# A convolution and top-2 mixture of experts on one core: opening rebuilt with a banded convolution, expert matmuls in 64-row pairs, and planned costs of GpSimd and of the row data changed

## The chip, the core and the metric

The kernel runs on one core of one Trainium2 chip, in one launch. The metric is the device time of an execution in microseconds (us). TensorE is called PE in the profile (its weight loads PEld), VectorE DVE, ScalarE ACT, GpSimd POOL and SyncE SP.

## The reference, cut to what matters

```
w   = softmax(weight, over the 7 taps)                 # 8 heads x 7 taps; a head is 24 of the 192 channels
xc  = causal convolution of x with w, per head         # x: 8 x 3584 x 192 f32, so N = 28672 tokens of D = 192
noisy = xc @ w_gate + log1p(exp(xc @ w_noise)) * noise # N x 8 experts
top2  = two largest of noisy, gates = softmax of those two
for e in range(8):                                     # F = 1024
    for each token that has e among its top two:
        out[token] += gate * (relu(xc[token] @ w1[e]) @ w2[e])
```

All inputs and outputs are f32. The kernel runs the expert matmuls in f16 on split operands: each value is scaled by a power of two and written as a high and a low f16 part, and three products (high by high, high by low, low by high) are summed in f32.

## The kernel before, in words

**Units.** The tokens fall into 28 units of 1024. In a unit each of the 128 partitions holds 8 neighbouring tokens, with the six tokens before them as the halo of the convolution. For each unit `load_x` (L278) brings 768 KB, `conv` (L545) makes xc, takes the largest absolute value of each row (L575), scales the rows by a power of two (L579) and writes the high and low parts into one of two row buffers `rb`, 400 f16 wide. `gating` (L594) then turns the rows into columns (on PE through the py buffers for the first five units, L613, by transposing DMAs for the others), multiplies them with the gate weights (the logits, L637, into the PSUM tile misc), and on DVE goes through some thirty small instructions of 64 columns: softplus, noise, two rounds of maximum and one-hot. M (L702) is the sum of both one-hots. PE ranks the rows of each expert with it (L709 and the two behind), DVE makes the row indices (idx, L747) and writes the gates into the row buffers. Last, `scatters` (L759) has GpSimd write the 1024 rows twice, in 16 indirect DMAs of 128 rows (L768), into a DRAM table xs that has a region for each expert.

**The convolution of the first units.** Units 0, 1 and 2 are convolved on PE (`conv_pe`, L501): one f32 matmul of 128 x 128 by 192 columns for each of 7 taps and each head (half of the heads of unit 0), with diagonal matrices `dg` that `diagonals` (L489) makes beforehand on DVE and ACT. ACT copies the result from PSUM (L569). All other units take DVE: a multiply and six multiply-adds for each of 8 heads, 56 instructions of 128 x 192 (L560, L562).

**Blocks.** A round takes the next rows of every expert: first a round of 128 rows, then 28 rounds of 256. A block is one expert in one round, so there are 232 blocks, of which 224 have 256 rows. For a block SP issues two transposing loads from xs (bT, three buffers; `block_loads`, L891). PE runs `mm1` (L848): for each half of F, 16 matmuls of 128 rows and 256 columns into a ph buffer (there are two), and four matmuls of 64 rows, which take the low part of the last 64 channels, at the end of the first half and at the start of the second. ACT writes the high part of the relu into h (L854), DVE the low part (`relu_low`, L858), and then ph is free. PE runs `mm2` (L866): for each 128 of the rows 24 matmuls of 192 columns into a py buffer (two). ACT scales by the gate (L872, y, six buffers), and GpSimd adds the rows to the output with an indirect DMA (L877). PE's order is mm1 of block n, then mm2 of block n-1. The row numbers and gates of a round come back from xs (`load_meta`, `round_meta`).

**What sets the order.** Each engine runs its instructions in the order in which the program lists them, and that list is written by a planner (class `Plan`, L46). The work is written as threads; a thread says `yield ENGINE, cost` before it emits instructions, and `run` (L90) always takes the thread whose start on the planned clock, less its urge, is smallest. The costs are written by hand: 1.05 for a scatter, 1.6 for an add, 0.33 for a conv step, 1.0 + 0.15 for a relu_low, 2.0 for an mm2 half. Rings (L499) stand for the buffers: 2 ph, 2 py, 6 y, 3 bT. Urges come from due times (L520 to L543). Semaphores, which keep the data right, are set independently of the plan.

**The opening.** Weights of expert 0 come first, then x of unit 1 and the other experts' weights in turn. Each expert's weights are scaled by a factor from the diagonal of their gram matrix (L364, matmuls into grams) and split in two (L412). The output is zeroed by 28 DMAs from SP (L432), one per unit. A block waits in the plan until every unit whose rows it may hold has scattered (`ready_unit`, L157).

Of the kernel before, what the change touches and what calls it, by code (L numbers as in the profile page):

```python
# [8 lines left out]
F32 = mybir.dt.float32  # L9
# [9 lines left out]
P = 128  # L19
# [26 lines left out]
class Plan:  # L46
# [7 lines left out]
    GAP = 0.1  # L54

    def __init__(self, **clock):
        self.clock, self.threads, self.now = clock, [], 0.0
# [32 lines left out]
    def run(self):  # L90
        self.spawned = []
        while True:
            best = None
            for th in self.threads:
# [3 lines left out]
                at = max(self.clock[eng], th[0] + (self.GAP if th[4] != eng else 0.0))  # L98
# [5 lines left out]
                urge = th[3](at) if callable(th[3]) else th[3]  # L104
                if best is None or at - urge < best[0]:
                    best = at - urge, at, th
# [18 lines left out]
def kernel(  # L125
# [22 lines left out]
    BIG = 2 * P  # L148
    assert D == 192 and E == 8 and I % TU == 0 and P % B == 0 and S % I == 0 and U > 3
# [28 lines left out]
    start = tc.tile_pool(name="start", bufs=1)  # L178
    spool = start.__enter__()
# [24 lines left out]
    def iota_f(name, shape, pattern, base, mult):  # L204
        t = const.tile(shape, I32, name=name + "_i")
        nc.gpsimd.iota(t, pattern=pattern, base=base, channel_multiplier=mult)
# [3 lines left out]

    tok0 = iota_f("tok0", [P, TU], [[1, TU]], 0, I)
    rowp = iota_f("rowp", [P, 2], [[P, 2]], 0, 1)
# [12 lines left out]

    runs = const.tile([P, U + 1, E], F32, name="runs")
# [3 lines left out]
    def pow2(mx, n, t, name):  # L230
# [8 lines left out]
        V.tensor_scalar(f, f, -1, 254, op0=OP.mult, op1=OP.add)  # L239
        V.tensor_scalar(i, f, 23, None, op0=OP.logical_shift_left)  # L240
        return s.bitcast(F32), i.bitcast(F32)
# [35 lines left out]

    def load_x(u):  # L278
        xt = xpool.tile([P, HALO + TU, D], F32, name="xt")
        xts[u] = xt  # L280
        if u:
            nc.sync.dma_start(xt[:, HALO:, :], dview(xf, u * TU * D, [[I * D, P], [D, TU], [1, D]]))
        else:
            for p0, p1 in ((16, P), (1, 16)):
# [781 lines left out]
```

## Time and profile before

| | before |
|---|---|
| median of 3 runs (lowest to highest) | 2117.39 us (2103.3 to 2119.4) |
| profiled execution | 2097.99 us |
| its span, first to last instruction | 2096.2 us |
| granted clock of PE, mean | 0.978 |
| busy: PE | 1983.7 us (95%) in 21703 matmuls |
| busy: DVE | 1565.0 us (75%) |
| busy: POOL | 1271.8 us (61%) |
| busy: ACT | 803.3 us (38%) |
| L848, mm1 | 9280 matmuls |
| L866, mm2 | 10944 matmuls |
| L858, relu_low | 557.5 us in 464 |
| L768, scatters | 494.2 us in 448 |
| L877, adds | 776.0 us in 456 |

How to read it: the profile is one execution. Busy time is the sum of what an engine's instructions lasted, so an engine can be busy 95% of the span and yet be held up in one part of it; the views by stretch show where. Matmuls overlap one another in the array, and a row of PE is a run of matmuls with its start, its length and their number. An idle time is written in brackets with what ended it: "<-DVE h L858" is a wait for a result, "<-issue" a time in which the engine waited for nothing that the trace shows. The granted clock is the share of its full clock that PE got.

### The profile page before, as it was taken

The page shows a single profiled execution, that of the slowest core. Times are in us where ns is not written, and L with a number is a line of the kernel's source. Part 1 is how long each engine was busy: PE and PEld are TensorE (multiplying, and loading weights), DVE is VectorE, ACT ScalarE, POOL GpSimd, SP SyncE. Part 2 cuts the span into 40 slices and gives each one's busy share as a digit, 9 for nine tenths or more (in the row PEclk, how much of TensorE's full clock was granted, in tenths as well). Part 3 has the DMA queues.
Part 4 walks back from the last instruction along what each step waited for, and adds up shares of the span by engine and source line. Part 5 has one row for each costly group of instructions (what it writes and reads, how often), then busy time and mean ns, then how long its engine had stood idle before and what let it go on. Part 6 is the DMA issues. An engine that isn't in the chain of part 4 may idle for free.

```text
span 2096.2 us, 52494 instructions
## 1 busy us (share of the span) xinstructions
PE 1983.7 (95%) x21703; PEld 1778.0 (85%) x21703; DVE 1565.0 (75%) x4042; ACT 803.3 (38%) x1173; POOL 1271.8 (61%) x915
## 2 busy tenths in 40 slices
PE   7557999999999999999999999999999999999997
PEld 6546888878888899889899998988898888999986
DVE  6677888878888898889988888889899753333232
ACT  4334343333334343443343434433443433333332
POOL 0353576765666776777667777777767665333333
PEclk9778999999999999999999999999999999999999
DMA  8733456876657677666777766677777664444442
GB/s 238 196 91 79 86 98 118 155 148 118 117 92 125 130 132 128 122 126 117 118 129 133 126 130 117 113 120 131 130 132 115 107 98 77 58 61 57 60 58 35
DMA packets 521882, 236.99 MB, mean 113 GB/s; under 512 B 401304, under 2 KB 508824, under 8 KB 521505
## 3 DMA queue, kind: packets, MB, share of 16 engines
q1 hardware_dynamic: 433824, 142.72, 33.2%
q0 software_dynamic: 87200, 90.80, 29.3%
q8 instruction: 171, 2.80, 0.6%
q14 instruction: 79, 0.65, 0.1%
q10 hardware_dynamic: 608, 0.02, 0.0%
HBM read 40.12 MB, written 115.38 MB: 74 GB/s over the span
## 4 chain that ended last, share of the span: by engine, by line
PE 88%; DVE 5%; issue 3%; SPq 2%; ACT 1%; DMA 1%; another core or an unknown queue 0%; ACTq 0%; POOL 0%; DVEq 0%; POOLq 0%
PE ph L848 43%; PE py L866 41%; PE ph L514 1%; SPq L622 1%; PE misc L637 1%; DVE h L858 1%; PE grams L364 1%; DVE xc L562 0%; DMA xT<-rb 0%; DVE w1s L412 0%; SPq L911 0%; DVE w2s L412 0%; PE py L613 0%; DVE t L673 0%
## 5 line engine op out<-in xcount | busy, mean ns | idle before, releaser
L877 POOL DMA_INDIRECT out_dram<-y,ids x456 | 776.0, 1702 | 593.2 <-ACT y L872 423.5
L848 PE MATMUL ph<-bT,w1s 128*128 128x256 f16 (+2 forms) x9280 | 1004.7, 273 | 26.6 <-issue 10.3
L866 PE MATMUL py<-w2s,h 128*128 128x192 f16 x10944 | 953.1, 246 | 12.0 <-issue 11.3
L848 PEld LDWEIGHTS <-w1s 128*128 128x128 f16 (+1 forms) x9280 | 773.2, 98 | 210.6 <-issue 116.6
L866 PEld LDWEIGHTS <-h 128*128 128x128 f16 x10944 | 910.0, 98 | 23.8 <-issue 18.3
L858 DVE SCALAR_TENSOR_TENSOR h<-ph,h 128x1024 f16<-128x1024 f32 (+1 forms) x464 | 557.5, 1203 | 389.8 <-ACT h L854 345.2
L854 ACT ACTIVATE h<-ph 128x1024 f16<-128x1024 f32 (+1 forms) x464 | 468.0, 1009 | 556.8 <-PE ph L848 469.1
L768 POOL DMA_INDIRECT xs<-rb,idx x448 | 494.2, 1103 | 212.7 <-issue 144.7
L562 DVE SCALAR_TENSOR_TENSOR xc<-xt,wt,xc 128x192 f32<-128x192 f32 x1224 | 422.9, 410 | 3.3 <-DMA xt<-zero 3.3
L872 ACT ACTIVATE y<-py,ga 128x192 f32<-128x192 f32 x456 | 191.5, 421 | 602.2 <-PE py L866 439.2
L514 PE MATMUL ph<-xt,dg 128*128 128x192 f32 x280 | 50.8, 339 | 14.9 <-DMA xt<-in_x_dram 11.6
L514 PEld LDWEIGHTS ph<-xt,dg 128*128 128x128 f32 x280 | 47.3, 197 | 15.3 <-DVE dg L494 11.5
L560 DVE TENSOR_SCALAR xc<-xt,wt 128x192 f32<-128x192 f32 x204 | 53.9, 330 | 1.2 <-DMA xt<-in_x_dram 0.5
L575 DVE TENSOR_REDUCE am<-xc 128x8 f32<-128x1536 f32 x28 | 49.0, 1752 | 4.4 <-ACT xc L569 3.7
L579 DVE TENSOR_TENSOR xc<-xc,xs 128x1536 f32<-128x1536 f32 x28 | 49.3, 1761 | 0.0
L637 PE MATMUL misc<-gparts,xT 128*128 128x32 f16 (+1 forms) x752 | 27.4, 175 | 16.7 <-issue 15.3
L673 DVE SCALAR_TENSOR_TENSOR t<-t,t 128x64 f32<-128x64 f32 x168 | 38.1, 227 | 5.7
L637 PEld LDWEIGHTS <-xT 128*128 128x128 f16 x752 | 24.4, 97 | 19.8 <-issue 17.6
L589 DVE TENSOR_TENSOR rb<-xc,rb 128x1024 f16<-128x1024 f32 x28 | 34.1, 1217 | 4.3 <-ACT rb L585 2.1
L585 ACT ACTIVATE rb<-xc 128x1024 f16<-128x1024 f32 x28 | 29.5, 1053 | 11.1 <-DVE xc L579 9.3
L483 ACT ACTIVATE xt<-xt 128x1152 f32<-128x1152 f32 x27 | 31.2, 1156 | 0.0
L719 DVE TENSOR_REDUCE sums<-M 128x72 f16<-128x576 f16 x23 | 27.0, 1172 | 0.0
(142 smaller groups left out, 620.0 us busy)
## 6 DMA issues: line engine op xcount, KB each, us to landing
out_dram<-zero SPq DMA_DIRECT2D x28, 768.0 KB
xt<-in_x_dram SPq DMA_DIRECT2D x27, 768.0 KB
bT<-xs SPq DMA_TRANSPOSE x464
out_dram<-y,ids POOLq DMA_INDIRECT x456
xs<-rb,idx POOLq DMA_INDIRECT x448
w2s<-in_moe_w_dram SPq DMA_DIRECT2D x16, 384.0 KB
w1s<-in_moe_w_dram SPq DMA_DIRECT2D x8, 512.0 KB
w1s<-in_moe_w_dram SPq DMA_DIRECT2D x16, 256.0 KB
```

Of the source, the lines that this page charges most:

```text
L514: nc.tensor.matmul(c[:, h - h0, :TU * G].rearrange("p (t g) -> p t g", g=G), diag[h, k], xts[u][:, k:k + TU, h * G:(h + 1) * G], start=(k ...
L560: V.tensor_scalar(dst, src, wt[:, h, k:k + 1], None, op0=OP.mult)
L562: V.scalar_tensor_tensor(dst, src, wt[:, h, k:k + 1], dst, op0=OP.mult, op1=OP.add)
L579: V.tensor_tensor(xc, xc, xsc[:, :, None].to_broadcast([P, TU, D]), op=OP.mult)
L637: nc.tensor.matmul(lg[:, t], xT[:, t, c, :], g[:, gc], start=(i == 0), stop=(i == len(seq) - 1))
L768: s = nc.gpsimd.indirect_dma_start(out=xsf, out_offset=bass.IndirectOffsetOnAxis(ap=idx[:, k, t:t + 1], axis=0), in_=rbf[:, t, :], in_offs ...
L848: nc.tensor.matmul(ph[:, f, :T], w, x, start=f // 2 not in banks[:i], stop=f // 2 not in banks[i + 1:], skip_group_check=True)
L854: nc.scalar.activation(h[:, 0, half * nf:(half + 1) * nf, :T], ph[:, :, :T], AF.Relu)
L858: V.scalar_tensor_tensor(h[:, 1, hs, :T], ph[:, :, :T], 0.0, h[:, 0, hs, :T], op0=OP.max, op1=OP.subtract)
L866: nc.tensor.matmul(py[:, :D], h[:, a, f, ts], w2_part(e, lo, f), start=(n == 0), stop=(n == 3 * FC - 1))
L872: nc.scalar.activation(y, py[:, :D], AF.Copy, scale=gate)
L877: a = nc.gpsimd.indirect_dma_start(out=out, out_offset=bass.IndirectOffsetOnAxis(ap=ids, axis=0), in_=y, in_offset=None, compute_op=OP.add)
```

## The change

**Pairs.** For blocks of 256 rows every matmul of 128 rows becomes two of 64 rows, one on the upper and one on the lower half of the array (`mm1_pairs`, `mm2_pairs`). In a first pass the upper half (partitions 0 to 63) works into one PSUM bank and the lower half into the other; in a second one (swap) the banks change places, so that each bank has both halves of the sum. Between the two an empty ACT instruction waits for the first pass, and the second pass waits for it (`passes`). PE's order is now: first pass of mm1 of block n (both ph buffers), first pass of mm2 of block n-1 (both py), second pass of mm1, second pass of mm2. Each product of mm1 is there as before; the four 64-row products of the last channels, that stood beside the others, are among the pairs of the first pass.

**Opening.** Units 0 to 3 lay out tokens otherwise: a partition holds single tokens, in four runs of 32 per slice (NB, RUN), so that the convolution runs along the partitions: for a head one 128-row f32 matmul of 192 columns with a band matrix and two 32-row ones of 96 columns for the halo, instead of seven with diagonals. The bands are made on DVE from seven flag matrices and predicated copies of the taps; the diagonals are gone, and with them the pool that block loads waited for. `conv_out` scales on DVE straight out of PSUM. The noise of these units comes in one load and a DVE transpose. The first 10 of unit 0's 16 scatters (HEAD = 5) are enough for the first round, and blocks go by groups of four experts (EARLY = 4): rounds 0 and 1 of experts 0 to 3, rounds 0 and 1 of experts 4 to 7, then the others as before. The weights of experts 0 to 3 come ahead of those of 4 to 7, units 2 and 3 are convolved between the first blocks, and the output rows of units 0 to 3 are zeroed by GpSimd's queue behind the weights of experts 1 and 2.

**Planner.** A scatter now counts 1.4 and an add 2.0. Row data come back 4.0 after their load (2.3 before), the transposed columns of units from 5 on after 5.0 (2.5), the counts of ranks 1.0 later. DRAIN adds 0.3 after a step on PE. A step that ends before the chosen one begins may go ahead of it (`able`). Due times count 57 per unit (UNIT) and the urge grows over 80 us (SLACK, 400 before). `ready_unit` takes 2.2 standard deviations instead of 3.0. The gates' values leave `gating` for a thread of their own (`gate_values`).

**Clock.** `keep_clock` fills PE's planned gaps over 0.5, up to 230 on the planned clock, with small f32 matmuls into a part of misc that nothing reads: 31, 7, 24, 20, 5, 26, 13 and 9 of them before the first block, about 247 in all.

The diff, cut to its core:

```diff
@@ class Plan @@
+    DRAIN = 0.3
...
-                at = max(self.clock[eng], th[0] + (self.GAP if th[4] != eng else 0.0))
+                gap = 0.0 if th[4] == eng else self.GAP + (self.DRAIN if th[4] == "PE" else 0.0)
+                at = max(self.clock[eng], th[0] + gap)
...
+            for one in able:
+                if one[2][1][0] == best[2][1][0] and one[1] + one[2][1][1] <= best[1]:
+                    if one[0] < best[0] or one[1] < best[1]:
+                        best = one
...
+            if self.fill and op[0] in self.fill:
+                self.fill[op[0]](self.clock[op[0]], at)
@@ rounds and blocks @@
+    NB, HR, EARLY = 4, 8, 4
+    HEAD = 5
+    blocks = [(j, e) for es in (range(EARLY), range(EARLY, E)) for j in range(2) for e in es]
+    blocks += [(j, e) for j in range(2, len(rounds)) for e in range(E)]
...
-            if mean * (u + 1) - 3.0 * sigma * math.sqrt(u + 1) >= end:
+            if mean * (u + 1) - 2.2 * sigma * math.sqrt(u + 1) >= end:
@@ zeros of the output @@
+    def zeros_first():
+        yield mark("weights", 1)
+        for u in range(NB):
+            zi = yield from zeros_of(u)
+            needs(zi, last_load[u // 2 + 1])
@@ def conv_pe @@
+                    if i is None:
+                        w, x = band[:, h], xts[u][:, HALO:, cols]
+                    else:
+                        w, x = band2[:NB * HR, h], halves(u)[i][:, :, cols]
+                        t0, t1 = i * TU // 2, (i + 1) * TU // 2
...
+                    nc.tensor.matmul(c[:, h - h0, t0 * G:t1 * G].rearrange("p (t g) -> p t g", g=G),
+                                     w.rearrange("p r j -> p (r j)"), x, start=b not in banks[:n],
+                                     stop=b not in banks[n + 1:], skip_group_check=True)
@@ due times @@
-    FIRST, EACH = 72.0, 8.1
+    FIRST, EACH, SLACK, UNIT, LEAD, FILLED = 72.0, 8.1, 80.0, 57.0, 12.0, 230.0
...
-        return 0.5 - max(-0.5, min(0.5, (t - at) / 400.0))
+        return max(0.0, min(0.9, 0.5 - (t - at) / SLACK))
@@ def gating @@
-                yield plan.now + 2.5
+                yield plan.now + 5.0
...
-                yield DVE, 0.7
+                yield DVE, 1.1
...
+                yield plan.now + 1.0
@@ def scatters @@
+        for v in range(max(u + 1, NB)):
+            yield mark("zeros", v)
...
-            yield POOL, 1.05
+            yield POOL, 1.4
...
+            if u == 0 and i == 2 * HEAD - 1:
+                done("scattered", "head", after=2.5)
...
-            slack = (due(u) - 40.0 - plan.now) / (2 * TU - i)
+            slack = (due(u) - 45.0 - plan.now) / (2 * TU - i)
             if u > 1:
-                yield plan.now + min(2.0, max(0.0, slack - 1.0))
+                yield plan.now + min(2.6, max(0.0, slack - 1.4))
@@ the passes @@
+    def passes(what, mm):
+        yield ACT, 0.1
+        passed[what] = nc.scalar.nop()
+        needs(passed[what], mm)
+        done("passed", what, mm.ins.name)
...
+    def mm1_pairs(e, xT, T, half, swap, ph):
+        nf = FC // 2
+        bank = [(f, f + nf // 2) if not swap else (f + nf // 2, f) for f in range(nf // 2)]
+        todo = []
+        for fs in bank:
+            for lo, wc, c in [(0, 0, 0), (1, 0, 0), (0, 0, 1), (0, 1, 2)]:
+                todo += [(f, w1_part(e, wc, lo, half * nf + f)[r], xT[r, c, :T]) for f, r in zip(fs, ROWS)]
...
+    def mm2_pairs(e, h, swap, pys):
+        todo = [(i, f, a, lo) for f in range(FC) for a, lo in ((0, 0), (0, 1), (1, 0)) for i in range(2)]
+        for n, (i, f, a, lo) in enumerate(todo):
+            t = 1 - i if swap else i
...
@@ def round_meta, results, run_blocks @@
-        yield plan.now + 2.3
+        yield plan.now + 4.0
...
-        yield POOL, 1.6
+        yield POOL, 2.0
...
-                yield PE, 0.1 + 1.96 * T / BIG, ph_ring
+                yield PE, 1.09 * T / BIG, ph_ring
...
+            plan.spawn(passes("ph", mm), 1.5)
+            if n:
+                yield from second(n - 1, False)
+            yield mark("passed", "ph", mm.ins.name)
+            for half in range(2):
+                yield PE, 0.88 * T / BIG
+                mm1_pairs(e, xTs[n], T, half, True, phs[half])
+                plan.spawn(evacuate(n, half, phs[half], T), 1.5)
```

**What this makes of the order.** First PE, in a round in the middle of the program: before, from the end of one block's mm2 into the next block. The names are the two ph and the two py buffers with running numbers, bT and h, and the weight slots w1s and w2s; in brackets stands the semaphore of the engine or queue that is waited for.

```order
L866 MATMUL py_16090<-w2s1_144,h_15855 128x192
L848 LDWEIGHTS w1s4_130 [waits DMAHW6_49]
L848 MATMUL ph_16132<-bT_15743,w1s4_130 128x256 [waits DVE_49]
...
L848 MATMUL ph_16166<-bT_15743,w1s5_131 128x256 [waits DVE_49]
...
L866 LDWEIGHTS h_15991 [waits Activation_49]
L866 MATMUL py_16192<-w2s2_145,h_15991 128x192 [waits Activation_49]
```

The same place now (L1052 is mm1_pairs, L1062 is mm2_pairs, Activation_sequencer the empty ACT instruction):

```order
L1052 MATMUL ph_13911<-bT_13389,w1s7_150 128x256
L1062 LDWEIGHTS h_13664 [waits Activation_49]
L1062 MATMUL py_13940<-w2s4_164,h_13664 128x192 [waits Activation_49]
L1062 MATMUL py_13941<-w2s4_164,h_13664 128x192 [waits Activation_49]
...
L1062 MATMUL py_13941<-w2s5_165,h_13664 128x192
L1052 LDWEIGHTS w1s6_149 [waits Activation_sequencer_49]
L1052 MATMUL ph_13877<-bT_13389,w1s6_149 128x256
...
L1052 MATMUL ph_13911<-bT_13389,w1s7_150 128x256
L1062 LDWEIGHTS h_13664 [waits Activation_sequencer_49]
L1062 MATMUL py_13941<-w2s4_164,h_13664 128x192
```

Both halves of ph and both of py are now open at once, and the passes of two neighbouring blocks take turns; before, the halves followed one another.

Second GpSimd, behind the opening: before, scatters of a unit (L768) and adds of blocks (L877).

```order
L877 DMA out_dram<-y,ids 28928x192 x2
L768 DMA xs<-rb_192,idx 287744x200 x5
L877 DMA out_dram<-y,ids 28928x192 x2
L768 DMA xs<-rb_192,idx 287744x200 x5
L877 DMA out_dram<-y,ids 28928x192 x2
L768 DMA xs<-rb_192,idx 287744x200
L877 DMA out_dram<-y,ids 28928x192 x6
```

Now its opening (L518 the zeros, L945 scatters, L1093 adds):

```order
L518 DMA out_dram<-zero 128x8x192 x4
L945 DMA xs<-rb_250,idx 287744x200 x16
L945 DMA xs<-rb_252,idx 287744x200 x13
L1093 DMA out_dram<-y,ids 28928x192
```

And behind it:

```order
L945 DMA xs<-rb_250,idx 287744x200 x3
L1093 DMA out_dram<-y,ids 28928x192 x2
L945 DMA xs<-rb_250,idx 287744x200 x3
L1093 DMA out_dram<-y,ids 28928x192 x2
L945 DMA xs<-rb_250,idx 287744x200 x2
```

Five scatters between two blocks' adds have become three or two; in the opening 29 scatters of units 0 and 1 stand in a row behind the zeros.

Third DVE, in the same rounds: before, single relu_low (L858) stood between the small instructions of a round's row data and gating.

```order
L562 SCALAR_TENSOR_TENSOR xc<-xt,wt,xc 128x8x24 x2
L858 SCALAR_TENSOR_TENSOR h<-ph,h 128x1024
L800 TENSOR_SCALAR lim<-runs 128x8
L804 TENSOR_TENSOR ok<-rowp,lim 128x16
...
L821 TENSOR_TENSOR ga<-ga,winv 128x16
L858 SCALAR_TENSOR_TENSOR h<-ph,h 128x1024
```

Now (L698 and L700 the convolution, L1074 relu_low):

```order
L698 TENSOR_SCALAR xc<-xt,wt 128x8x24 x2
L700 SCALAR_TENSOR_TENSOR xc<-xt,wt,xc 128x8x24 x9
L1074 SCALAR_TENSOR_TENSOR h<-ph,h 128x1024 x2
L700 SCALAR_TENSOR_TENSOR xc<-xt,wt,xc 128x8x24 x17
L1074 SCALAR_TENSOR_TENSOR h<-ph,h 128x1024 x2
```

The two relu_low of a block now stand together, and up to 17 steps of the convolution stand between two such pairs.

More of the change, by code (lines that the diff above doesn't have):

```diff
@@ L366 @@
     wscale = {}
+    groups = (0,), (1, 2), (3, 4), (5, 6), (7,)
     def scale_weights():
-        for es in ((0,), (1, 2), (3, 4), (5, 6), (7,)):
+        for i, es in enumerate(groups):
             n, turn["scale"] = len(es), es[0]
+            for m in range(2 if i > 1 else 0):
+                yield mark("split", groups[i - 2][-1], m)
             for e in es:
@@ L478, in halos @@
     def halos():
-        for u in range(1, U):
+        done("halo", NB)
+        for u in range(NB + 1, U):
             yield mark("x", u - 1)
@@ L539, in wanted, with block_at @@
+    turn = {"conv": 0, "pe": 0, "out": 0, "gating": 0, 0: 0, 1: 0, "scale": 0}
+    def block_at(e):
+        return block_time(next(i for i, b in enumerate(blocks) if b[1] == e))
     def wanted(what, ahead):
-        return lambda at: by(due(turn[what]) - ahead, at)
+        return lambda at: by(due(turn[what]) - ahead, at) if turn[what] else 1.5
     def wanted_weights(what, ahead):
@@ L605, in gating @@
             if u < NTR:
-                for t in range(0, 3 * TU, 8):
+                for c in range(3):
+                    yield mark("part", u, c)
                     yield PE, 0.6, py_ring
@@ L831, in loads @@
                     needs(ld, s)
-        waited.update(range(ready[j] + 1))
+        waited.update(u for u in scat if u <= ready[j])
         tc.add_to_no_dep_group("loads", ld.ins)
@@ L985, in run_blocks, with keep_clock @@
             if n:
-                yield from second(n - 1)
-        yield from second(len(blocks) - 1)
-    plan = Plan(PE=0.0, DVE=6.7, ACT=5.7, SP=5.5, POOL=13.0)
-    plan.now = 2.5
-    first = [(h, k) for h in range(HH) for k in reversed(range(K))]
+                yield from second(n - 1, True)
+        for swap in (False, True):
+            yield from second(len(blocks) - 1, swap)
+    def keep_clock(a, b):
+        for _ in range(int(0.75 * (min(b, FILLED) - a) / 0.25) if b - a > 0.5 else 0):
+            nc.tensor.matmul(misc[:, 384:496], ones32, ident[:, :112], start=True, stop=True)
+    plan = Plan(PE=1.0, DVE=11.0, ACT=10.0, SP=4.5, POOL=9.0)
+    plan.fill[PE] = keep_clock
+    plan.now = 4.5
     plan.spawn(loads_first(), 0.6)
-    plan.now = 6.0
-    plan.spawn(diagonals(first[0::3] + first[1::3], DVE), 0.5)
-    plan.spawn(diagonals(first[2::3] + [(h, k) for h in range(HH, H) for k in reversed(range(K))], ACT))
+    plan.spawn(zeros_first(), 0.3)
+    plan.now = 10.5
     plan.spawn(halos(), 0.3)
-    plan.spawn(conv_pe(), 0.2)
+    plan.spawn(conv_pe(), wanted("pe", 80.0))
+    plan.spawn(conv_out(), lambda at: 1.5 if turn["out"] == 0 else 1.0)
     plan.spawn(conv(), wanted("conv", 70.0))
     plan.spawn(prepare_gates(), 0.3)
-    plan.spawn(scale_weights(), wanted_weights("scale", 12.0))
+    plan.spawn(scale_weights(), wanted_weights("scale", 25.0))
     for m in range(2):
-        plan.spawn(split_weights(m), wanted_weights(m, 6.0))
+        plan.spawn(split_weights(m), wanted_weights(m, 10.0))
     plan.spawn(gating(), wanted("gating", 45.0))
```

517 lines of the change are left out of this document (341 added, 176 removed).

## The prediction, made before the changed kernel was run

> **What bounds the kernel now.** I read the busy time by stretch first, since the whole-span share (PE 95%) averages an opening with a main phase. The columns are the stretch, its length, then busy time (and instructions) of PE, PEld, DVE, ACT and POOL, the granted clock, the DMA share and GB/s.
>
> ```profile
> 0.00:100.00 100.00, 64.91 (x546) 61.78 (x547) 64.35 (x237) 39.32 (x72) 18.03 (x27) 0.89 0.83 225
> 100.00:200.00 100.00, 62.11 (x695) 53.37 (x693) 74.07 (x205) 38.45 (x52) 46.29 (x39) 0.75 0.31 72
> 200.00:700.00 500.00, 480.54 (x5255) 423.33 (x5253) 427.66 (x1143) 193.97 (x280) 327.80 (x229) 0.99 0.66 121
> 700.00:1600.00 900.00, 894.73 (x9954) 804.55 (x9952) 795.91 (x2092) 356.87 (x522) 641.93 (x456) 1.00 0.71 123
> ```
>
> From 200 us on PE is the bound, with DVE next (795.91 of 900). Before 200 us PE idles and runs at 0.75 to 0.89 of its clock. Between 200 and 700 us PE idles 19.5 us, in the 900 us after that only 5.3. Next the chain that ended last (page, then its pieces): PE holds 88%, nearly all in the two expert matmul lines, and the full 256-row blocks begin at 198.62.
>
> ```profile
> PE 88%; DVE 5%; issue 3%; SPq 2%; ACT 1%; DMA 1%; another core or an unknown queue 0%; ACTq 0%; POOL 0%; DVEq 0%; POOLq 0%
> 198.62 4.14 PE ph L848 x40
> ```
>
> Then PE's timeline over one block, and four cuts of it around the 64-row matmuls of mm1 (a row takes the shape of its first matmul; that of 1004.54 holds the last full one and the first pair).
>
> ```profile
> 1002.90 4.31 PE L848 MATMUL ph<-bT,w1s 128*128 128x256 f16 x40
> 1007.05 4.12 PE L866 MATMUL py<-w2s,h 128*128 128x192 f16 x48
> 1011.01 1.25 PE L848 MATMUL ph<-bT,w1s 128*128 128x256 f16 x10
> ...
> 1004.22 0.49 PE L848 MATMUL ph<-bT,w1s 128*128 128x256 f16 x3
> 1004.54 0.49 PE L848 MATMUL ph<-bT,w1s 128*128 128x256 f16 x3
> 1004.75 0.50 PE L848 MATMUL ph<-bT,w1s 64*128 64x256 f16 x6
> 1005.09 0.49 PE L848 MATMUL ph<-bT,w1s 64*128 64x256 f16 x3
> ```
>
> One matmul lasts 0.27 us, so three in 0.49 start 0.109 apart: a full slot. Six 64-row ones fit in 0.50: they run two at a time, a pair per slot. Between the last full matmul (1004.54) and the first pair (1004.75) lie 0.21, and 0.20 between the last pair (1005.09) and the next full one: each change of shape costs 0.10. mm2 takes 3.96 for 48, 0.0825 each. A block is 8.11.
>
> **The change part by part.** *64-row pairs.* A block now has 36 pairs of 0.109 in mm1 and 48 pairs of 0.0825 in mm2: 7.89 us instead of 8.11. So the slots are the same, and what goes is two changes of shape: 0.217 x 224 blocks = 48 us. Given back: logits and ranks remain 128-row and were free among 128-row blocks; now each group is two changes, two groups in each of 28 units: 28 x 2 x 0.2 = 11. Net 37. What it asks of PE's queue is 336 instructions (loads and matmuls) in 7.89 us, 23.5 ns each, against 46 now. The trace bounds that: 40 small matmuls and the grams behind them.
>
> ```profile
> 44.14 1.16 PE L637 MATMUL misc<-gparts,xT 128*128 128x16 f16 x40
> 45.16 1.19 PE L364 MATMUL grams<-w1s 128*128 128x128 bf16 x16
> 46.98 0.54 PE L514 MATMUL ph<-xt,dg 128*128 128x192 f32 x2
> ```
>
> 68 matmuls with 68 loads start between 44.14 and 46.98: 21 ns each. The price lies between 21 and 46 ns; I take that 23.5 is met, nearest to the first row. The Trainium skill, "TensorE: Matmul & The Clock Gate", section "Wait — 56ns, not 53.3ns?", says that without hardware decode a matmul costs the sequencer about 62 ns and that this binds once the array needs less; 168 x 62 ns would be 10.4 us a block and the sum 2580. The row above speaks against it (25 ns each with their loads), though part of it may have waited in a filled queue.
>
> *The wait for the swap.* The second pass waits for an empty instruction on ACT, and behind it in ACT's order stand that block's relu and y. It has the whole other pass (1.98 us) to come back, so 0; without that cover it is some 0.5 us a block. The real price is that ph is held longer. These rows are one block late in the program:
>
> ```profile
> 1803.68 4.31 PE L848 MATMUL ph<-bT,w1s 128*128 128x256 f16 x40
> 1805.96 1.02 ACT L854 ACTIVATE h<-ph 128x1024 f16<-128x1024 f32 x1 [1.66 <-PE ph L848]
> 1807.02 1.22 DVE L858 SCALAR_TENSOR_TENSOR h<-ph,h 128x1024 f16<-128x1024 f32 x1 [3.95 <-ACT h L854]
> 1808.03 1.02 ACT L854 ACTIVATE h<-ph 128x1024 f16<-128x1024 f32 x1 [1.04 <-PE ph L848]
> ```
>
> mm1 ends its slots at 1807.83, ACT begins at 1808.03. So from a half's last slot to ph free: 0.2 + 1.02 + 0.04 + 1.22 + about 0.1 = 2.6 us. Before, the next use of that buffer was 6 us away; now it is the other half's second pass and mm2's (0.87 + 1.98 = 2.85). The spare is some 0.25 us. DVE is 88% busy there:
>
> ```profile
> L858 DVE SCALAR_TENSOR_TENSOR h<-ph,h 128x1024 f16<-128x1024 f32 x241 | 294.1, 1222 | 67.3 <-ACT h L854 51.3 <-issue 12.2 <-ACT rb L585 0.9
> L562 DVE SCALAR_TENSOR_TENSOR xc<-xt,wt,xc 128x192 f32<-128x192 f32 x783 | 270.7, 410 | 0.0
> ```
>
> The new DVE order puts up to 17 conv steps between two pairs of relu_low. Overlapped, one is 270.7 / 783 = 0.346, so 17 of them and the pair (2.44) are 8.3 us, against a block of 7.89. Three or four of a round's eight blocks are that full, the others not. Bounds: 0 (all in the spare) and 0.5 a block; I take 0.09 on average, 20 us, nearer to the first since most windows have room.
>
> *GpSimd planned longer.* The scatter now counts 1.4 and the add 2.0 instead of 1.05 and 1.6. What PE pays for crowding stands here: PE at 450 us, behind five scatters in a row, and in the opening behind sixteen.
>
> ```profile
> 74.90 0.17 PE L637 MATMUL misc<-gparts,xT 128*128 128x16 f16 x1 [0.49 <-issue]
> 75.62 0.23 PE L637 MATMUL misc<-gparts,xT 128*128 128x16 f16 x3 [0.55 <-issue]
> 77.03 0.25 PE L637 MATMUL misc<-gparts,xT 128*128 128x16 f16 x4 [1.18 <-issue]
> ...
> 450.95 0.33 PE L866 MATMUL py<-w2s,h 128*128 128x192 f16 x2 [0.24 <-issue]
> 451.67 0.24 PE L866 MATMUL py<-w2s,h 128*128 128x192 f16 x1 [0.39 <-issue]
> 453.82 0.48 PE L866 MATMUL py<-w2s,h 128*128 128x192 f16 x2 [1.18 <-issue]
> ```
>
> PE gets one to four instructions each 0.7 us and waits for nothing that the trace shows. In the order of before this region has five scatters between two adds; from 750 us on one to three, and PE is full. The new order has three throughout after the opening. So 200 to 700 should idle as 700 to 1600 does: 19.5 - 2.9 = 17, and 3 for the clock (0.99): 20. Three scatters and two adds, each with the 0.3 us gap before it, are 3 x 1.4 + 2 x 2.05 = 8.3, over 7.89, but only in five of eight blocks; the six y buffers carry that, so 0. The bounds are 0 and 25.
>
> *The opening.* These rows carry it: gating of unit 0 from z to M, its indices, its 1st and 16th scatter, the load behind them, and PE.
>
> ```profile
> 45.34 0.28 DVE L658 SCALAR_TENSOR_TENSOR z<-misc,ginv,xi 128x64 f32<-128x64 f32 x1 [1.19 <-PE misc L637]
> 57.73 0.22 DVE L702 TENSOR_TENSOR M<-oh,oh 128x64 f16<-128x64 f32 x1
> 62.89 0.17 DVE L747 CAST idx<-idxf 128x16 int32<-128x16 f32 x1
> 64.00 1.06 POOL L768 DMA_INDIRECT xs<-rb,idx  x1 [52.22 <-ACT xc L569]
> 83.99 0.97 POOL L768 DMA_INDIRECT xs<-rb,idx  x1 [0.30 <-issue]
> 87.65 0.37 SPq L788 DMA_DIRECT2D mt<-xs  x1
> 96.73 0.21 PE L709 MATMUL misc<-M,before 128*128 128x64 f16 x1 [11.69 <-DVE M L702]
> 97.06 4.23 PE L848 MATMUL ph<-bT,w1s 128*128 128x128 f16 x40
> ```
>
> New unit 0: flags, memsets and seven predicated copies stand before the bands. No row has them at this size; between the 0.2 us of a 64-column and the 1.2 us of a 1024-column DVE instruction I put 8 us, so bands at about 15. Eight heads of 0.7 (f32 rows above: two passes of 192 columns in 0.35) end at 20; reduce, scale, split, transposes and logits 10; z to M 8 (12.4 with 4.6 of other work between); rank, idx and gates 4: indices at 42 instead of 63. Scatters are 1.275 apart (64.00 to 83.99), the head has 10 of 16, so the load comes 16 us behind the first instead of 23.6: 58, and with two transposing loads behind it block 0 could start at about 63. But its place on PE is behind unit 1's rank, and unit 1's logits fall under unit 0's sixteen scatters, where PE crawls (the rows at 75 us). I take them as free at 63, M ten later: blocks 0 to 3 from about 77 (now 97), unit 1's scatters 77 to 97, four experts of 256-row blocks from 104. From there PE is dense; now from 198.6. At 104 the new kernel still owes four 128-row blocks (4 x 4.2 = 17), two convs, four grams and two units' logits (25), of which the old one at 198.6 owes 2. Gain 94.6 - 42 + 2 = 55; bounds 10 (dense at 150) and 65 (dense at 95). The zero writes on POOL wait for the weights of experts 1 and 2 and stand before the scatters: some 7.5 MB at 225 GB/s (first row) are in by 38 us, so 0; ten us later they would be the wait. The clock-keeping matmuls fill planned gaps only: 0, and up to 0.25 us each where a gap is missing. Crowded scatters behind the opening: -10.
>
> **Sum.** 55 + 37 + 20 - 20 - 10 = 82. The profiled execution took 2097.99 us (span 2096.2): 2016. The median of the runs, 2117.39, is 1.0092 of that execution: 2034.
>
> **Rivals.** *Ring* (slower side): PE waits for ph at each block. For it: spare of 0.25 us and DVE at 88%; against: pairs of relu_low stand adjacent and most windows have room. At 0.5 us a block it is 92 more: 2127. It decides from 0.45 us a block on. *Instruction rate* (far slower): PE takes no instruction in less than, say, 30 ns over a whole block (between 21 and 46): 10.1 us a block, 490 more, 2530; it eats the gain from 25.2 ns on. Against it is the row of 44.14. The rule of the Trainium skill named above is this rival's, with its own price. *Opening stuck*: PE crawls under both bursts, 29 scatters on end, dense only at 150: 46 more, 2081. *All of it*: no wait on DVE, dense at 95: 29 less, 2005. That pairs don't run side by side is excluded by the row of 1004.75.
>
> **How the numbers follow.** The sum's case 0.53 (own range 1990 to 2070), all of it 0.22, opening stuck 0.12, ring 0.08, instruction rate 0.05. The range 1965 to 2100 leaves out the two slower ones and the tail below 2005. About 1% is what a measurement of this kernel tells from no change. Faster by over 1% (under 2096): nearly all of the first two and most of the third, 0.83; within 1%: part of the third and the ring, 0.08; slower 0.09.
>
> **What would show it.** A block of 7.9 us in PE's timeline with no 0.21 gap inside mm1; PE's first full block near 77 and no gap over 3 us after 104; idle by "issue" at 200 to 700 below 6 us; DVE as the releaser of ph for about 20 us in all. Wrong would be: blocks over 8.1 us, PE waiting on DVE h or on ACT's empty instruction for over 100 us, or "issue" gaps inside pairs.

## The result, and the profile after

| | before | changed |
|---|---|---|
| median of 4 runs each (lowest to highest) | 2114.63 us (2103.3 to 2119.4) | 2341.02 us (2337.26 to 2352.47) |
| ratio, 95% interval | | 1.1088 (1.1028 to 1.1148) |
| span of the profiled execution | 2096.2 us | 2339.5 us |
| granted clock | 0.978 | 0.963 |

The change made the kernel slower by 11%, where 4% faster was forecast. Busy time by stretch, changed kernel (columns as in the prediction: PE, PEld, DVE, ACT, POOL, clock, DMA share, GB/s):

```profile
0.00:100.00 100.00, 72.82 (x673) 66.93 (x674) 60.49 (x241) 18.59 (x25) 35.62 (x55) 0.85 0.65 165
100.00:200.00 100.00, 82.32 (x1114) 73.82 (x1114) 59.42 (x159) 36.28 (x47) 23.75 (x21) 0.89 0.56 136
200.00:700.00 500.00, 451.39 (x8785) 412.52 (x8783) 369.19 (x963) 168.50 (x255) 297.21 (x205) 0.97 0.61 105
700.00:1600.00 900.00, 818.70 (x16042) 750.59 (x16038) 675.94 (x1755) 293.89 (x451) 572.50 (x388) 0.98 0.62 108
```

The loss is in the main phase, where PE was full before: of 900 us it now idles 81.3 (5.3 before), of the 500 ahead of them 48.6 (19.5). DVE, ACT and POOL all fell, so none of them is the new bound. What PE waited for (total, times, longest):

```profile
PE py L1062 <- issue: 87.5, 209, 1.4
PE ph L1052 <- issue: 67.7, 153, 1.3
PE misc L783 <- issue: 12.0, 16, 1.6
PE ph L1052 <- DVE h L1074: 10.8, 24, 0.8
PE ph L1052 <- ACTq L1035: 7.1, 1, 7.1
```

Before, the same two matmul lines waited so:

```profile
PE py L866 <- issue: 11.3, 25, 1.2
PE ph L848 <- issue: 10.3, 25, 1.2
```

"issue" means that the trace shows nothing waited for. The wait for ph, the prediction's slow-side rival, is 10.8 us in all. The empty ACT instruction (ACTq L1035) is named once, for 7.1 us in the opening. Next stands PE's timeline over two blocks, then GpSimd in the same time:

```profile
1005.78 1.94 PE L1052 MATMUL ph<-bT,w1s 64*128 64x256 f16 x32
1007.53 1.68 PE L1062 MATMUL py<-w2s,h 64*128 64x192 f16 x36
1009.53 0.24 PE L1062 MATMUL py<-w2s,h 64*128 64x192 f16 x1 [0.32 <-issue]
1010.23 0.27 PE L1062 MATMUL py<-w2s,h 64*128 64x192 f16 x2 [0.46 <-issue]
1010.94 0.57 PE L1062 MATMUL py<-w2s,h 64*128 64x192 f16 x9 [0.45 <-issue]
1011.29 2.41 PE L1052 MATMUL ph<-bT,w1s 64*128 64x256 f16 x40
1013.48 2.20 PE L1062 MATMUL py<-w2s,h 64*128 64x192 f16 x48
1015.46 1.97 PE L1052 MATMUL ph<-bT,w1s 64*128 64x256 f16 x32
```

```profile
1006.55 0.99 POOL L945 DMA_INDIRECT xs<-rb,idx  x1 [1.24 <-DVE rb L919]
1007.85 0.99 POOL L945 DMA_INDIRECT xs<-rb,idx  x1 [0.30 <-issue]
1009.14 0.96 POOL L945 DMA_INDIRECT xs<-rb,idx  x1 [0.30 <-issue]
1012.25 2.09 POOL L1093 DMA_INDIRECT out_dram<-y,ids  x1 [2.14 <-ACT y L1088]
```

Where nothing disturbs it, the pairs run as forecast: 40 in 2.19, 48 in 1.98, 32 in 1.75. But some 2.6 us behind the first of three scatters PE stops, takes one, two, nine matmuls at 0.7 us intervals, and goes on 0.8 us after the third scatter has ended. Beside the add that follows here there is no gap. That is the crawl that the prediction had seen in the opening and behind five scatters.

Counted over the whole trace (a gap: two neighbouring matmuls start more than 0.22 us further apart than the columns of the first take, and their whole spacing is counted; a run: scatters less than 0.6 us apart, with the gaps up to 1 us behind the last of them; block times go from one mm1 start to the next):

| behind 200 us | before | changed |
|---|---|---|
| gaps in all | 45.6 us | 290.8 us |
| runs of 2 scatters, mean gaps | 109, 0.10 us | 41, 0.70 us |
| runs of 3 | 5, 0 | 96, 1.97 us |
| runs of 5 | 11, 1.06 us | 0 |
| block with no scatter, fastest and median | 8.10, 8.10 us | 7.89, 8.13 us |
| block with three scatters, median | 8.10 us | 9.70 us |

There are 75 gaps before and 448 now. Some 0.09 us of each is the columns' own time, so by this estimate the idle part is 39 and 251 us. These 212 us more are most of the loss (2339.5 - 2096.2 = 243.3).

In the opening the same thing happens: scatters of unit 1 stand from 88.07 to 105.2, and the first block falls under them.

```profile
93.18 0.80 PE L1052 MATMUL ph<-bT,w1s 64*128 64x128 f16 x21
94.46 0.29 PE L1052 MATMUL ph<-bT,w1s 64*128 64x128 f16 x4 [0.48 <-issue]
95.19 0.21 PE L1052 MATMUL ph<-bT,w1s 64*128 64x128 f16 x1 [0.44 <-issue]
...
100.17 0.30 PE L1052 MATMUL ph<-bT,w1s 64*128 64x128 f16 x2 [0.96 <-issue]
107.54 1.89 PE L1052 MATMUL ph<-bT,w1s 64*128 64x128 f16 x32 [7.06 <-ACTq L1035]
```

The last row is the 7.1 us: the first pass ends at 100.47, and the empty instruction comes at 107.5, though ACT had been idle since 92.2. In the same kernel on a chip without the crawl (after_again, below) this wait does not appear in the opening; why ACT came late isn't shown.

Counting columns times rows of all expert matmuls, the work of four 256-row blocks was done at 195.2 us (200.4 before), that of eight at 254.2 (236.1 before).

### The profile page after: what moved, and what is told of

The parts are those of the page before. It is cut to its first block, busy times and chain, and to the rows that moved or that the text cites. A ratio compares the mean times of both kernels' runs of the same rounds, so it can differ in the third digit from the quotient of the medians.

```text
span 2339.5 us, 89819 instructions
## 1 busy us (share of the span) xinstructions
PE 2103.0 (90%) x40242; PEld 1942.8 (83%) x40242; DVE 1549.3 (66%) x3993; ACT 747.3 (32%) x1130; POOL 1315.9 (56%) x934
## 5 line engine op out<-in xcount | busy, mean ns | idle before, releaser
L1093 POOL DMA_INDIRECT out_dram<-y,ids x456 | 827.2, 1814 | 795.9 <-ACT y L1088 592.9
L1062 PE MATMUL py<-w2s,h 64*128 64x192 f16 x21504 | 1054.2, 246 | 92.5 <-issue 87.5
L1052 PE MATMUL ph<-bT,w1s 64*128 64x256 f16 (+1 forms) x16704 | 1046.4, 271 | 89.6 <-issue 67.7
L1062 PEld LDWEIGHTS <-h 64*128 64x128 f16 x21504 | 935.2, 95 | 157.2 <-issue 151.4
L1052 PEld LDWEIGHTS <-w1s 64*128 64x128 f16 x16704 | 883.9, 95 | 163.6 <-issue 129.0
L1074 DVE SCALAR_TENSOR_TENSOR h<-ph,h 128x1024 f16<-128x1024 f32 (+1 forms) x464 | 542.5, 1202 | 575.9 <-ACT h L1070 481.5
L1070 ACT ACTIVATE h<-ph 128x1024 f16<-128x1024 f32 (+1 forms) x464 | 448.8, 1006 | 891.4 <-PE ph L1052 818.3
L945 POOL DMA_INDIRECT xs<-rb,idx x448 | 479.3, 1070 | 178.2 <-issue 149.9
L700 DVE SCALAR_TENSOR_TENSOR xc<-xt,wt,xc 128x192 f32<-128x192 f32 x1152 | 394.0, 410 | 0.0
L1088 ACT ACTIVATE y<-py,ga 128x192 f32<-128x192 f32 x456 | 167.6, 418 | 340.4 <-PE py L1062 191.2
L1237 PE MATMUL misc<-ident,ones 128*128 128x112 f32 x446 | 66.2, 313 | 10.3 <-DVE wf L466 4.7
L1237 PEld LDWEIGHTS misc<-ident,ones 128*128 128x128 f32 x446 | 62.4, 225 | 12.3 <-DVE wf L466 5.0
L698 DVE TENSOR_SCALAR xc<-xt,wt 128x192 f32<-128x192 f32 x192 | 49.9, 328 | 0.7
L789 DVE TENSOR_TENSOR lgs<-misc,lgs 128x128 f32<-128x128 f32 x23 | 6.7, 290 | 48.6 <-ACT lgs L787 42.3
```

The lines of the kernel that those rows point to most:

```text
L698: V.tensor_scalar(dst, src, wt[:, h, k:k + 1], None, op0=OP.mult)
L700: V.scalar_tensor_tensor(dst, src, wt[:, h, k:k + 1], dst, op0=OP.mult, op1=OP.add)
L945: s = nc.gpsimd.indirect_dma_start(out=xsf, out_offset=bass.IndirectOffsetOnAxis(ap=idx[:, k, t:t + 1], axis=0), in_=rbf[:, t, :], in_offs ...
L1052: mm = nc.tensor.matmul(ph[:, f, :T], w, x, start=not swap and i < 2, stop=swap and i >= len(todo) - 2, skip_group_check=True)
L1062: mm = nc.tensor.matmul(pys[t][:, :D], h[ROWS[i], a, f, t * P:(t + 1) * P], w2_part(e, lo, f)[ROWS[i]], start=not swap and n < 2, stop=swa ...
L1070: nc.scalar.activation(h[:, 0, half * nf:(half + 1) * nf, :T], ph[:, :, :T], AF.Relu)
```

## The experiments

**Theories.** *Supply*: while GpSimd runs indirect scatters back to back, PE is handed hardly any instructions and lives on a store; pairs double the instructions of a block, so the store ends in 2 to 3 us instead of 6 to 9. *Array*: the pairs themselves stall (two row halves at once, the second passes, held ph). *Planner*: the new order of GpSimd and the rebuilt opening do it, whatever the matmuls.

**A bare measurement, and three part changes.** *micro* has no convolution and no experts; this is its stream, and the scatter:

```
            elif form == "cols":
...
                nc.tensor.matmul(t[:, :128], w, xx[:, :128], start=True, stop=True, skip_group_check=True)
            else:
                r, c = slice(64 * (i % 2), 64 * (i % 2) + 64), 256 if form == "pairs" else 64
                nc.tensor.matmul(t[:, :c], w[r], xx[r, :c], start=True, stop=True, skip_group_check=True)
...
        s = nc.gpsimd.indirect_dma_start(out=xsf, out_offset=bass.IndirectOffsetOnAxis(ap=idx[:, i:i + 1], axis=0),
                                         in_=zero[:, :cols], in_offset=None)
```

> This kernel computes nothing of the reference: it zeroes the output and then runs ten phases, each a stream of PE matmuls beside one kind of work on GpSimd, which begins some 8 us after the stream. Supply theory (GpSimd's scatters cut off PE's supply of instructions; PE lives on a store of 100 to 130 of them): full 128-row matmuls beside 16 scatters stay dense for about 6 us of the run and then crawl at one to four instructions each 0.7 us until it ends; 64-row pairs crawl 2 to 3 us after the first scatter; 128-row matmuls of 128 columns, which have the pairs' rate of instructions without pairs, crawl as early as the pairs; pairs beside index-making instructions, or beside nothing, have no gap over 0.2 us; scatters held 1 us apart cost less than half as much each. Array theory (the pairs themselves are what stalls): the pairs have gaps beside nothing as well, and the 128-column matmuls go like the full ones.

*whole* keeps all of the change but the pairs:

```diff
-                yield PE, 1.09 * T / BIG, ph_ring
-                phs.append(psum.tile([P, FC // 2, BIG], F32, name="ph", bufs=2))
+                yield PE, 0.1 + 1.96 * T / BIG, ph_ring
...
-                mm = mm1_pairs(e, xTs[n], T, half, False, phs[half])
+                plan.spawn(evacuate(n, half, mm1(e, xTs[n], T, half), T), 0.6)
```

> The changed kernel with full 128-row matmuls and the order of blocks of before; the new opening, planner and GpSimd costs stay. Supply theory: a block is 8.1 us again, runs of three scatters cost below 0.1 each instead of 1.97, and the execution takes 2095 to 2125 us. Planner theory (the new order of GpSimd, with scatters three in a row, starves PE): the runs of three still cost 1 us and more, and it takes 2230 or more. Array theory: 2095 to 2125 as well.

*pairs_only* is the kernel of before with `passes`, `mm1_pairs`, `mm2_pairs` and the new `second` and `run_blocks`, and nothing else of the diff.

> The kernel of before with the pairs alone. Supply theory: dense blocks of 7.9 us, but its runs of two scatters cost 0.7 each and those of four and five 3 to 4 instead of 0.5 and 1.1: about 2180 us (2150 to 2230). Planner theory: the pairs' own gain and nothing else, 2061. Array theory: the whole loss is here, about 2300.

*split_cols* cuts the matmuls of before in columns:

```diff
-            nc.tensor.matmul(ph[:, f, :T], w, x, start=f // 2 not in banks[:i], ...)
+            for k in range(2):
+                cs = slice(k * T // 2, (k + 1) * T // 2)
+                nc.tensor.matmul(ph[:, f, cs], w, x[:, cs], start=f // 2 not in banks[:i] and k == 0, ...)
```

> The kernel of before with each expert matmul cut into two of half the columns: 128 rows as before, no pairs, no second pass, but twice the instructions. Supply theory: dense blocks near 8.1 us with no scatter, and the starving of pairs in runs of scatters: about 2240 us (2190 to 2300). Array theory: no starving, about 2100.

These four ran on another chip, and there the kernel of before took 2037.3 us (2027.79 to 2046.41), not 2115. micro had no gap over 0.3 us in its first nine phases, pairs beside 16 scatters included. whole took 2021.66, ratio 0.9916 (0.989 to 0.9942); pairs_only 2227.88, 1.0913 (1.0854 to 1.0972); split_cols 2095.27, 1.0259 (1.0203 to 1.0316). No trace of the four has the crawl. So on this chip supply theory missed three numbers (micro, whole, split_cols); pairs_only fell into its 2150 to 2230, but by luck, since the wait there is another one (below). Array theory told split_cols' 2095 and missed the other three. The first question became whether starving is a matter of the chip. A chip that shows no such gaps is called calm from here on.

pairs_only shows what then holds PE, here for a reason of its own:

```profile
PE ph L873 <- DVE h L895: 150.5, 27, 17.7
```

With the planner of before, DVE's relu_low is late by up to 17.7 us while both ph are held: the prediction's ring rival, in full. split_cols' fastest block is 8.31 us: twice the instructions cost 0.21 a block without any starving.

**The changed kernel on a calm chip.** *after_again* is the changed kernel, *micro2* is micro, *whole2* is whole, and *whole_no_clock* is whole with

```diff
-    plan.fill[PE] = keep_clock
+    plan.fill[PE] = lambda a, b: None
```

> The changed kernel as it stands, beside before on one chip. The first set of runs had before at 2115 us with gaps of "issue" on PE, a second set on another chip had it at 2037 and, in the kernels run there, no such gap. Supply theory: where a chip shows no such gaps, this kernel has blocks of 7.9 us and takes 1985 to 2020 us, faster than before; where it shows them, 2300 and more. Array theory: slower than before by about 10% on either.

> The ten phases once more, on the chip of the other kernels of this set. If after_again starves here: full matmuls crawl some 6 us into the 16 scatters, pairs and 128-column matmuls 2 to 3 us into them, and nothing crawls beside GpSimd's index-making or beside nothing. If it does not: no gap over 0.3 us in any of the first nine phases.

> The changed kernel with full matmuls once more, beside the changed kernel itself. Supply theory: on a chip that starves, 200 us and more faster than after_again, its runs of three scatters below 0.1 us each; on one that does not, some 20 to 40 us slower than after_again, since its blocks are 8.1 and not 7.9. Planner theory: as slow as after_again on a chip that starves.

> The changed kernel with full matmuls, and without the small matmuls that fill PE's planned gaps. If they keep the clock up in the opening: 5 to 10 us slower than whole2, with a granted clock below 0.8 in the first 200 us. If they only sit in gaps: within 3 us of it. If they take instructions that PE lacks: faster.

On this second calm chip (before 2044.93) after_again took 2052.17, ratio 1.0039 (1.0004 to 1.0075). Its timeline has no gap of issue:

```profile
1007.75 2.35 PE L1052 MATMUL ph<-bT,w1s 64*128 64x256 f16 x40
1009.93 2.15 PE L1062 MATMUL py<-w2s,h 64*128 64x192 f16 x48
1011.91 1.91 PE L1052 MATMUL ph<-bT,w1s 64*128 64x256 f16 x32
1013.66 2.15 PE L1062 MATMUL py<-w2s,h 64*128 64x192 f16 x48
1015.64 2.35 PE L1052 MATMUL ph<-bT,w1s 64*128 64x256 f16 x40
```

From 1007.75 to 1015.64 is the block of 7.89. Runs of three scatters cost 0.07 us each here (1.97 on the first chip), and the same program is 289 us shorter. Still it isn't faster than before: the 1985 to 2020 expected were missed. whole2 beside it took 2029.08, ratio 0.9935 (0.9908 to 0.9962): it was expected 20 to 40 us slower than after_again and was 23 faster. The stretch 700 to 1600, after_again and then whole2:

```profile
700.00:1600.00 900.00, 874.81 (x18418) 832.37 (x18415) 779.15 (x2046) 334.16 (x517) 663.37 (x448) 0.99 0.74 123
```

```profile
700.00:1600.00 900.00, 900.00 (x10030) 810.95 (x10028) 804.13 (x2095) 360.68 (x526) 657.83 (x459) 1.00 0.72 125
```

Full matmuls leave no idle time at all; pairs leave 25.2 us, about what 0.21 a block saves in 111 blocks (23). Of these, 9.9 us are waits for DVE's relu_low, 8.9 for a py that ACT had not yet read, and 4.4 one wait for the empty ACT instruction. And the pairs' opening is later: eight blocks of work are done at 215.6 against 199.5. Up to there the small clock-keeping matmuls hold PE for 68.2 us in after_again (428 records) and 54.3 in whole2 (344), while the gaps differ little (23.7 and 20.1). These matmuls fill what the plan leaves free, so it is the plan with pairs that leaves PE more to fill; that it does so because two ph are taken at a time is argued, not shown. whole_no_clock has 0.9933 (0.989 to 0.9975): the 0.76 of the clock in its first 100 us, against 0.85, can't be told in the time.

**All forms in one program.** *mixed* takes the form by the round (`"one" if j == 0 else ("pairs", "full", "halves")[j % 3]`) and ends with micro's ten phases.

> The changed kernel with three forms of expert matmuls by turns: rounds 3, 6, 9 and so on in 64-row pairs, rounds 1, 4, 7 full, rounds 2, 5, 8 full but cut into two halves of the columns; behind its end stand the ten phases of matmuls beside GpSimd's work (they add zeros and change nothing). On a chip that starves as in the first runs, supply theory: rounds of pairs and of halves, which both have twice the instructions, lose 1.5 to 2 us per run of three scatters, full rounds below 0.2; in the phases the crawl as told for them. Array theory: the pairs alone lose. Planner theory: all three lose alike. On a chip that does not starve: pairs near 7.9 us a block, full 8.1, halves 8.3, no loss in runs of scatters in any.

It met a chip that starves (before 2118.45 beside it; one execution of each). Between 260 us and the end of the blocks, a block's worth of full matmuls took 8.45 us, of pairs 9.56, of halves 9.86; runs of three scatters had 0.11 us of gaps in full rounds (23 runs), 1.90 in pairs (24) and 1.81 in halves (39). Halves are 128-row matmuls with no second pass, so array theory falls; the three stand under one planner and one kind of GpSimd order, so planner theory falls as the cause of the main loss. In the groups by shape the idle time stands at the end of each row:

```profile
L1086 PE MATMUL py<-w2s,h 128*128 128x192 f16 x4032 | 351.8, 247 | 4.8 <-issue 4.3
L1064 PE MATMUL py<-w2s,h 64*128 64x192 f16 x6912 | 335.7, 246 | 30.8 <-issue 28.2 <-ACTq L1037 0.5
L1086 PE MATMUL py<-w2s,h 128*128 128x96 f16 x6912 | 333.3, 208 | 54.9 <-issue 53.6
```

Its phases tell what starves. Each row is PE beside one kind of work on GpSimd (columns as in the prediction, matmuls in the first brackets), from the first instruction of that work on: pairs beside nothing; beside 16 scatters full matmuls, pairs, halves; pairs beside 16 scatters of 32 bytes a row, beside eight scatters with 1 us between, beside ten adds, beside index-making:

```profile
2300.00:2320.00 20.00, 20.00 (x372) 17.53 (x368) 0.00 (x0) 0.00 (x0) 1.16 (x3) 1.00 0.01 2
2338.50:2358.50 20.00, 12.80 (x103) 9.82 (x101) 0.00 (x0) 0.00 (x0) 15.43 (x16) 0.88 0.22 78
2391.80:2411.80 20.00, 9.40 (x98) 4.86 (x95) 0.00 (x0) 0.00 (x0) 15.40 (x16) 0.66 0.22 78
2445.90:2465.90 20.00, 9.24 (x100) 6.34 (x97) 0.00 (x0) 0.00 (x0) 15.38 (x16) 0.67 0.22 78
2500.70:2520.70 20.00, 10.29 (x98) 4.65 (x94) 0.00 (x0) 0.00 (x0) 15.41 (x16) 0.67 0.03 4
2555.00:2572.00 17.00, 17.00 (x318) 15.15 (x314) 0.00 (x0) 0.00 (x0) 15.74 (x17) 1.00 0.15 51
2589.70:2608.00 18.30, 18.30 (x340) 16.32 (x336) 0.00 (x0) 0.00 (x0) 15.55 (x11) 1.00 0.49 51
2622.00:2642.00 20.00, 20.00 (x372) 17.84 (x368) 0.00 (x0) 0.00 (x0) 18.71 (x20) 1.00 0.01 2
```

Beside scatters 1.28 us apart PE gets about 100 matmuls in 20 us whatever their form. Full ones first lack instructions after 9.3 us and 168 matmuls and loads, pairs after 3.2 and 114, halves after 3.6 and 120. (Supply theory had told some 6 us for full ones and a store of 100 to 130; so the store, if it is one, has no fixed size.) Rows of 32 bytes do the same as rows of 800, so it isn't the bytes. Scatters 2.16 us apart do nothing, so for scatters it is how close they stand. Adds 1.86 apart do nothing either, but no row has adds at 1.28; and 15 plain DMAs of GpSimd in 8.08 us leave PE without a gap. The calm chip's micro2, pairs beside 16 scatters:

```profile
172.70:192.70 20.00, 20.00 (x372) 17.86 (x368) 0.00 (x0) 15.27 (x17) 1.00 0.22 74
```

**Scatters apart.** *after_spaced* and *whole_spaced* (with whole3 beside them) put time between the scatters:

```diff
+            for _ in range(2 if u else 0):
+                nc.gpsimd.iota(idle, pattern=[[1, 320]], base=0, channel_multiplier=1)
```

> The changed kernel with two index-making instructions on GpSimd, some 0.35 us each, behind each scatter of units 1 to 27, and the scatter planned at 2.1. Supply theory: with scatters 2 us apart PE is not starved, so on a chip that starves (before above 2100) the gaps of issue behind 200 us fall from 290 to below 60 us and the execution from 2341 to 2100 or less, unless GpSimd itself becomes the bound (two adds and two scatters a block are 7.8 us of 7.9). On a chip that does not starve: no faster than the 2052 of the unspaced kernel there, up to 60 slower. Array theory: the gaps stay.

> The same spacing with full matmuls. Supply theory: on a chip that starves 10 to 30 us faster than whole3, all of it in the opening and in the few runs of four and more; on one that does not, the same or up to 20 slower, since the scatters take longer.

> The changed kernel with full matmuls once more. On a chip that starves supply theory expects 2095 to 2125 us beside some 2115 of before, since full rounds lost 0.1 us per run of three scatters there; planner theory 2230 and more. On a chip that does not: 0.992 of before, as twice measured.

The chip was calm (before 2041.56). after_spaced took 2239.45, ratio 1.0978 (1.0933 to 1.1022), whole_spaced 1.0901 (1.0856 to 1.0946), whole3 0.99 (0.9862 to 0.9938). Up to 60 us more than after_again's 2052 and up to 20 more than whole3 were expected; it became 187 and 203, because GpSimd became the bound. after_spaced, one block of it:

```profile
1000.92 1.62 POOL L1097 DMA_INDIRECT out_dram<-y,ids  x1 [1.64 <-ACT y L1092]
1002.84 1.56 POOL L1097 DMA_INDIRECT out_dram<-y,ids  x1 [0.30 <-issue]
1004.71 0.99 POOL L947 DMA_INDIRECT xs<-rb,idx  x1 [0.30 <-issue]
1005.71 0.88 POOL L951 IOTA idle<- 128x320 int32 x2
1006.75 0.99 POOL L947 DMA_INDIRECT xs<-rb,idx  x1 [0.17 <-issue]
1007.75 0.88 POOL L951 IOTA idle<- 128x320 int32 x2
1009.06 1.61 POOL L1097 DMA_INDIRECT out_dram<-y,ids  x1 [0.43 <-issue]
```

Two adds and two scatters are 8.14 us without a pause, more than a block, and a third scatter with its two fillers (2.04) makes it 10.2. So filling GpSimd's time is no cure; whether spacing would help on a chip that starves was not met.

**Full matmuls on a chip that starves.** *whole4* and *whole5* are whole again, to meet such a chip.

> The changed kernel with full matmuls, for a chip that starves (before above 2100 us beside it). Supply theory: 2095 to 2125, the runs of three scatters at 0.1 us each, ratio to before 0.99 to 1.005. Planner theory: 2230 and more. On a chip that does not starve: 0.99 of before, as measured three times.

> As for whole4: on a chip that starves supply theory expects 2095 to 2125 and a ratio of 0.99 to 1.005, planner theory 2230 and more; on one that does not, 0.99 of before.

whole4 met a calm one: 2020.94, ratio 0.9921 (0.9887 to 0.9955). whole5 met one that starves (before 2115.57): 2124.28, ratio 1.0038 (1.0011 to 1.0065). Supply theory's 2095 to 2125 holds, just; without the pairs the loss of 11% is 0.4%. Its groups of expert matmuls:

```profile
L1027 PE MATMUL ph<-bT,w1s 128*128 128x256 f16 (+2 forms) x9280 | 1008.8, 272 | 39.0 <-issue 29.5 <-DVE h L1074 5.6 <-DMA bT<-xs 1.7
L1082 PE MATMUL py<-w2s,h 128*128 128x192 f16 x10944 | 949.5, 246 | 12.1 <-issue 11.0 <-ACT y L1088 0.2
```

Runs of three scatters cost 0.21 us there (109 runs), twice the 0.1 told. All gaps behind 200 us are 85 us against 45.6 of before, so the rest of the change starves PE a little too, and its earlier opening (eight blocks of work at 221.5 against 236.1) about pays for that. With full matmuls most of it comes late: 55 of the 85 us, and 27 of the 45.6 before, fall while an add is GpSimd's latest instruction, most of them within 3 us of the last scatter. Why PE lacks instructions beside those adds, when adds alone did nothing, isn't shown.

## Why the prediction was wrong

- **Pairs, dense block of 7.89 us**: right, to the second figure, for the fastest block on either kind of chip; the median block without a scatter is 8.13 on the first chip. The empty ACT instruction, taken as 0, cost 7.1 us once in the opening, and 4.4 us once in after_again; the 0.5 us a block that it was to cost without cover comes from no row.
- **Ring, 20 us**: right in kind, 10.8 and 11.9 us. pairs_only shows that it is the new planner that keeps it so small (150.5 without).
- **"I take that 23.5 is met"**: this step failed. In a dense stretch it is met: 336 instructions in 7.89 us. It isn't met behind scatters, and the prediction had the rows for that: it priced "one to four instructions each 0.7 us" as a cost of five scatters and more, and called three in a row full. That holds at the 22 instructions a microsecond of before. With twice as many the supply lasts a third as long (3.2 against 9.3 us in mixed), and three in a row, which the new order has throughout, become the worst place instead of the cure. The two terms, pairs and GpSimd's order, were priced apart, and what they did together was the result: 96 runs x 1.97 = 189 us, and 41 x 0.70 = 29.
- **GpSimd planned longer, +20**: wrong in sign on chips that starve. 200 to 700 idles 48.6 us with pairs; with full matmuls (whole5) 21.3, against 19.5 before, and 700 to 1600 idles 25.9 there, against 5.3. The six y buffers were taken to carry GpSimd's work at no cost; in after_again ACT waited 21.4 us for adds to free a y, and PE 12.5 us for ACT to free a py.
- **Opening, +55**: four blocks of work 5 us earlier, eight blocks 18 us later. Unit 0's indices were ready at 48.5 us (42 forecast, 63 before). The row of unit 1's logits under unit 0's scatters was read and taken as free at 63 us; the crawl lasted to 73.5, M came at 83.0 (73 forecast), and block 0 began at 93.18 (77 forecast) under unit 1's scatters, which stand from 88.07 on. Without pairs the opening is worth 14.6 us at eight blocks (221.5 against 236.1), so the size was wrong as well.
- **Instruction rate rival, 2530**: nearest to the outcome, but by another mechanism: no limit over a whole block. (It would have eaten the gain of 82 us from 24.6 ns an instruction on, not from 25.2: 7.89 + 82 / 224 = 8.26 us over 336.) In mixed, small matmuls came 128 at a time with their 128 loads, at 2688.88, 2692.36 and 2696.12 us, with "issue" between: 256 instructions in 3.6 us, 14 ns each, less than the pairs ask for. The Trainium skill, "TensorE: Matmul & The Clock Gate", section "Wait — 56ns, not 53.3ns?", gives some 62 ns for a matmul where hardware decode is off. That price wasn't met in micro2, where 297 small matmuls and 295 loads took 6.00 us, 20 ns from matmul to matmul; whether hardware decode was on no run shows:

```profile
425.40:431.40 6.00, 5.92 (x297) 5.80 (x295) 0.00 (x0) 5.79 (x4) 0.72 0.02 5
```

- On the calm chips the mechanism "pairs save 0.21 a block" is there, and is given back by waits (25.2 us in 900) and by the opening: 1.0039. The forecast of 4% failed there by the opening's size, and by taking the pairs' cost in waits at 20 us for the whole run. Without pairs the change was worth 16 to 22 us on the calm chips (whole to whole4), where the opening and GpSimd's order were priced at 55 + 20 - 10 = 65.

## What to carry to other kernels

A gap that the profile puts down to "issue" has a rate in it: ask how many instructions the engine ate before it began, and what the change does to that number; a change that doubles an engine's instructions must be priced at the places where their supply is thin, not at the dense ones. Price two terms together where one draws on what the other fills. And before a few per cent are believed, look at the kernel of before on the same chip: here it took 2028 to 2051 us on four chips and 2103 to 2127 in the three other sets of runs, and a change that costs 11% on the one kind costs 0.4% on the other.

## What the runs showed of the hardware

- Sets of runs differ: beside scatters 1.28 us apart PE crawled in three of them (before at 2114.63, 2118.45 and 2115.57) and not in four others (2037.3, 2044.93, 2041.56, 2038.72), with the same programs. Those whose chip is on record were each on another chip, so chip and moment can't be told apart; that it is the chip is argued, not shown.
- What holds the instructions isn't shown. PE's stream comes in blocks of 16 KB (queue q8: 171 of them for 43406 instructions before, 316 for 80484 changed, so about 256 to a block):

```profile
q8 instruction: 316, 5.18, 0.9%
```

 In mixed's crawl of pairs one such block had landed just ahead, and none moved for the next 19 us, in which PE ran fewer than 100 instructions; so a block that comes late isn't what the trace shows there. Nor do the blocks take longer: at the median 1.04 us in the changed kernel's first trace and 1.08 in after_again's. Why some sets of runs crawl, and whether recording the trace has a part in it, no run here can tell.
- Pairs of 64-row matmuls on two halves of the array run at the slot of one full matmul, loads included, as long as instructions come: 48 of them in 1.98 us are 24 pairs of 0.0825, as long as one full matmul of 192 columns took before.
